# Fixing the order of the tensor engine's instructions in an mLSTM cell followed by a two-layer tanh-shrink block

## Chip, cores and metric

One core of one Trainium2 chip. The metric is the device time of one execution in microseconds (us); times quoted are medians of several executions, and a "span" is the length of the one execution that the profile shows. PE is the tensor engine, PEld its weight loads, DVE, ACT and POOL are the vector, scalar and GpSimd engines.

## The reference

```python
def _attn_ref(q, k, v, i_gate, f_gate, o_gate):          # q, k, v: (4, 8, 768, 40)
    for t in range(S):                                   # ... gates f, i stabilised by a running maximum m
        C = f_stab * C + i_stab * outer(v[t], k[t])      # per batch and head
        n = f_stab * n + i_stab * k[t]
        y[t] = sigmoid(o_gate[t]) * (C @ q[t]) / max(abs(n @ q[t]), 1)

def _moe_ref(x, w_in, w_out):                            # x: (3072, 320), w_in: (320, 2048), w_out: (2048, 320)
    h = x @ w_in
    return (h - np.tanh(h)) @ w_out                      # x is y with heads joined to 320 columns
```

The weights reach the kernel as 64-bit numbers, and it turns them into 32-bit ones itself.

## The kernel before

The cell is done in 24 units of 128 tokens (6 chunks of 128 time steps for each of 4 batches). A unit has, on PE, 8 `scores` calls (tile `ps`), 8 `update` calls of the state (`pc`), 8 `product` pairs (`ph`) and 3 transposes (`px`, which give `xT`). The dense part works on groups of two units: 12 groups of 8 pairs of w_in columns, 6 calls a pair (`ph_up`) and 4 calls of w_out (`po`). The profile has two records a call, except for transposes. `merge` interleaves a quarter of a cell slot with a pair of the dense part by their estimated cost.

```python
V, A, G, T = nc.vector, nc.scalar, nc.gpsimd, nc.tensor
# ...
def weights(dst, src):                    # one piece: 3 pieces a block of w_in, 2 of w_out
    # ... load of 64-bit words, split into lo and hi
    V.tensor_single_scalar(e, hi, 0x7FF00000, op=OP.bitwise_and)
    A.activation(out=e, in_=e, func=AF.Relu, scale=8.0, bias=rebias[0:p])
    V.tensor_single_scalar(m, hi, 12, op=OP.logical_shift_left)
    A.activation(out=mf, in_=m.bitcast(U32), func=AF.Copy, scale=2.0 ** -32, bias=1.0)
    A.activation(out=rf, in_=lo, func=AF.Copy, scale=2.0 ** -52)
    G.tensor_tensor(out=rf, in0=rf, in1=mf, op=OP.add)
    G.tensor_tensor(out=rf, in0=rf, in1=e.bitcast(FP), op=OP.mult)
    V.scalar_tensor_tensor(out=dst.bitcast(I32), in0=hi, scalar=-(1 << 31), in1=r,
                           op0=OP.bitwise_and, op1=OP.bitwise_or)
# ...
xT = [const.tile([128, NK, TG], FP, name=f"xT{i}") for i in range(2)]
# ...
def inter(n):
    def update(h):
        # ...
        T.matmul(t["pc"][:, h, :], t["k"][:, h, :], t["vs"][:, h, :], start=True, stop=True)
    # ...
        steps += [(0.08, lambda h=h: update(h)) for h in range(H)]
# ...
AHEAD = GT + 2
EARLY = 3
for s in range(AHEAD):
    merge(cell_slot(s), convert(s) if s < EARLY else [])
for x in range(len(pairs) + LAG):
    # ... a quarter of a cell slot in `cell`; conversion of block p + EARLY while g == 0
    dense += up(g, p)                     # 6 calls on w_in
    dense += down(*pairs[x - LAG])        # 4 calls on w_out
    merge(dense, cell)
```

The order in the source is not the order that runs: the framework's scheduler reorders each engine's instructions within the dependencies.

Of the kernel before, what the change touches and what calls it, by code (L numbers as in the profile page):

```python
# [34 lines left out]
NO_SYNC = mybir.DependencyInfo(mybir.DependencyClass.NoSync, mybir.DependencyReason.DATA)  # L35
# [14 lines left out]
def kernel(  # L50
# [11 lines left out]
    out: bass.AP,  # L62
):
    nc = tc.nc
    V, A, G, T = nc.vector, nc.scalar, nc.gpsimd, nc.tensor

    B, NT, D, H, _ = qT.shape
    D1 = D + 1
# [91 lines left out]
    for dst, w in ((eS, after), (eT, ones)):  # L160
        p = ps_b.tile([dst.shape[0], NT, BH], FP, name="psum_lf", tag="b")
        T.matmul(p.rearrange("p c n -> p (c n)"), w, lfT.rearrange("p c n -> p (c n)"),
                 start=True, stop=True)
# [158 lines left out]
    def output(n):  # L322


        def accumulate(out, lhsT, rhs, last):
            t = un[n]
            i = T.matmul(out, lhsT, rhs, start=not t["mm"], stop=last, skip_group_check=True)  # L327
            if t["mm"]:
                tc.add_manual_dep(i.ins, t["mm"][-1].ins.name, NO_SYNC, reason="order within a bank")
            t["mm"].append(i)  # L330

        def product(h):
            t = un[n]
            if h == 0:
                t["ph"] = ps_b.tile([L, H, D1], FP, name="ph", tag="b")
                t["mm"] = []
            if t["c"]:
                old = state[t["b"]][t["c"] % 2]
                accumulate(t["ph"][:, h, :], t["qg"][:, h, :], old[:, h, :], False)
            accumulate(t["ph"][:, h, :], t["P"][:, h, :], t["vw"][:, h, :], True)  # L340
            if h == H - 1:
                close()

        def close():
            t = un[n]
            ph, sg = t["ph"], t["o"]
            A.activation(out=sg, in_=sg, func=AF.Sigmoid)

            den = att.tile([L, H], FP, name="den", tag="den")
            V.tensor_scalar(out=den, in0=ph[:, :, D], scalar1=-1.0, scalar2=1.0, op0=OP.mult, op1=OP.max)  # L350
            V.tensor_tensor(out=den, in0=den, in1=ph[:, :, D], op=OP.max)
            V.reciprocal(out=den, in_=den)
            G.tensor_tensor(out=sg, in0=sg, in1=den.unsqueeze(2).to_broadcast([L, H, D]), op=OP.mult)
            y = t["y"] = ys[n % 2]
            V.tensor_tensor(out=y[:, 0:DM].rearrange("p (h d) -> p h d", d=D), in0=ph[:, :, 0:D], in1=sg, op=OP.mult)

        return [(0.44 if n // B else 0.22, lambda h=h: product(h)) for h in range(H)]

    def turn(n):
# [160 lines left out]
```

## Time and profile before

| | before |
|---|---|
| time, median of 4 runs | 745.6 us (744.2 to 745.8) |
| span of the profiled run | 743.2 us |
| PE busy | 674.0 us, 91% |
| last of the 24 w_in pieces converted | 173.2 us |
| PE continuous from | 182.9 us |
| first of the last two output copies starts | 739.3 us, then 3.9 us of tail |

How to read it: before about 183 us PE waits again and again for weights, after it once, for 0.4 us. The prediction below shows the lines. What it and the text below call PE's end (739.3 us) is the start of the first of the last two output copies; by the profile's model PE's last call runs on to 739.8.

### The profile page before, as it was taken

What the parts mean: (1) busy time and instruction counts of PE and PEld (TensorE: products, weight loads), DVE (VectorE), ACT (ScalarE), POOL (GpSimd) and SP (SyncE); (2) the same over time, 40 slices, a digit from 0 to 9 for tenths busy, and PEclk for the clock granted to TensorE, in tenths of its full rate; (3) what the DMA queues carried; (4) which work ended last, traced back from release to release, by engine and by line L of the source; (5) the groups of instructions that cost most, each with busy time, mean ns of one, the idle gap of its engine ahead of it and who ended that gap; (6) DMA issues with size and microseconds to landing.
All of it is one profiled execution on the core that took longest, in us unless ns stands there. A gap on an engine that the chain in (4) does not pass through costs nothing.

```text
span 743.2 us, 9593 instructions
## 1 busy us (share of the span) xinstructions
PE 674.0 (91%) x3418; PEld 531.1 (71%) x3418; DVE 505.5 (68%) x823; ACT 308.7 (42%) x584; POOL 211.5 (28%) x230
## 2 busy tenths in 40 slices
PE   3387756687999999999999999999999999999997
PEld 2375645475787787787787787787787888888885
DVE  8775897488967566666666666666666775656665
ACT  4435644344544334333333333333333444344453
POOL 6467665764011320320320320320320220100000
PEclk8557986679999999999999999999999999999999
DMA  6444544245102121221221111222121000000000
GB/s 187 138 132 136 160 126 129 77 155 158 54 13 79 33 68 54 62 67 53 64 66 54 64 64 54 65 69 76 55 73 37 19 18 27 1 19 1 0 19 18
DMA packets 26487, 50.95 MB, mean 69 GB/s; under 512 B 3304, under 2 KB 15976, under 8 KB 26440
## 3 DMA queue, kind: packets, MB, share of 16 engines
q1 hardware_dynamic: 22568, 46.21, 20.7%
q10 hardware_dynamic: 3872, 4.13, 1.6%
q8 instruction: 27, 0.44, 0.3%
q14 instruction: 20, 0.16, 0.1%
HBM read 46.20 MB, written 4.13 MB: 68 GB/s over the span
## 4 chain that ended last, share of the span: by engine, by line
PE 78%; POOL 9%; DVE 7%; issue 4%; ACT 2%; ACTq 0%; DVEq 0%; POOLq 0%
PE ph_up L401 34%; PE po L430 27%; PE ph L327 9%; PE ps L295 4%; POOL w_r L230 4%; POOL w_r L229 3%; PE pc L309 3%; PE px L367 1%; DVE w_e L223 1%; POOL vw L278 1%; ACT w_m L227 1%; DVE w_in L231 1%; POOL qg L276 1%; DVE w_out L231 1%; ACT w_e L224 1%
## 5 line engine op out<-in xcount | busy, mean ns | idle before, releaser
L401 PE MATMUL ph_up<-xT,w_in 128*128 128x256 f32 x1152 | 325.9, 398 | 17.9 <-DVE w_in L231 15.9
L430 PE MATMUL po<-w_out,gt 128*128 128x320 f32 x768 | 260.6, 454 | 10.7 <-DVE gt L421 8.0
L401 PEld LDWEIGHTS ph_up<-xT,w_in 128*128 128x128 f32 x1152 | 201.6, 194 | 51.4 <-DVE w_in L231 17.0
L413 ACT ACTIVATE z<-ph_up 128x512 f32<-128x512 f32 x96 | 57.3, 597 | 310.4 <-PE ph_up L401 308.6
L430 PEld LDWEIGHTS po<-w_out,gt 128*128 128x128 f32 x768 | 136.2, 194 | 45.3 <-DVE gt L421 8.8
L417 DVE SCALAR_TENSOR_TENSOR w<-ph_up,z 128x512 f32<-128x512 f32 x96 | 65.9, 686 | 118.2 <-ACT t L414 118.2
L295 PEld LDWEIGHTS ps<-qT,kT 128*128 128x128 f32 x384 | 71.9, 223 | 34.8 <-DVE P L297 18.1
L295 PE MATMUL ps<-qT,kT 128*128 128x128 f32 x384 | 74.7, 311 | 24.0 <-DVE P L297 17.3
L308 POOL TENSOR_TENSOR state<-state,eT 40x328 f32<-40x328 f32 x16 | 14.3, 895 | 238.8 <-PE ph L327 232.0
L421 DVE COPY_PREDICATED gt<-big,t 128x512 f32<-128x512 int32 x96 | 74.7, 778 | 7.2
L327 PE MATMUL ph<-vw,P 128*128 128x41 f32 x384 | 77.0, 302 | 0.5 <-ACT xT L369 0.5
L420 DVE SCALAR_TENSOR_TENSOR gt<-q,w 128x512 f32<-128x512 f32 x96 | 72.5, 755 | 5.0 <-DVE den L350 0.4
L327 PEld LDWEIGHTS ph<-state,qg 128*128 128x128 f32 x320 | 61.5, 197 | 15.7 <-POOL w_r L230 1.0
L415 ACT ACTIVATE q<-z,square 128x512 f32<-128x512 f32 x96 | 69.3, 722 | 0.0
L416 ACT ACTIVATE big<-z,border 128x512 f32<-128x512 f32 x96 | 69.0, 719 | 0.0
L419 DVE SCALAR_TENSOR_TENSOR w<-z,w 128x512 f32<-128x512 f32 x96 | 66.9, 697 | 0.0
L418 DVE TENSOR_TENSOR t<-ph_up,t 128x512 f32<-128x512 f32 x96 | 65.3, 680 | 0.0
L278 POOL TENSOR_TENSOR vw<-v,eiT 128x320 f32<-128x320 f32 x24 | 25.4, 1059 | 138.5 <-PE ph L327 92.9
L327 PEld LDWEIGHTS ph<-vw,P 128*128 128x128 f32 x384 | 62.8, 214 | 1.2 <-ACT xT L369 0.9
L414 ACT ACTIVATE t<-ph_up 128x512 f32<-128x512 f32 x96 | 56.8, 592 | 1.6 <-DVE gt L421 1.6
L273 DVE TENSOR_TENSOR_SCAN E<-F,diag 128x1024 f32<-128x1024 f32 x24 | 57.3, 2388 | 0.0
L297 DVE TENSOR_TENSOR P<-ps,E 128x512 f32<-128x512 f32 x48 | 32.5, 682 | 32.7 <-PE ps L295 31.9
(80 smaller groups left out, 528.7 us busy)
## 6 DMA issues: line engine op xcount, KB each, us to landing
F<-f_rows SPq DMA_DIRECT2D x24, 512.0 KB
w<-in_moe_w_out SPq DMA_DIRECT2D x16, 320.0 KB
w<-in_moe_w_in SPq DMA_DIRECT2D x16, 256.0 KB
qT<-in_qT SPq DMA_DIRECT2D x24, 160.0 KB
kT<-in_kT SPq DMA_DIRECT2D x24, 160.0 KB
v<-in_v SPq DMA_DIRECT2D x24, 160.0 KB
k<-in_k SPq DMA_DIRECT2D x24, 160.0 KB
o<-in_o_gate SPq DMA_DIRECT2D x24, 160.0 KB
```

The source lines that it names most:

```text
L273: V.tensor_tensor_scan(out=E.rearrange("p h t -> p (h t)"), data0=t["F"].rearrange("p h t -> p (h t)"), data1=diag.rearrange("p h t -> p ( ...
L295: T.matmul(t["ps"][:, j, :], t["kT"][:, h, :], t["qT"][:, h, :], start=True, stop=True)
L327: i = T.matmul(out, lhsT, rhs, start=not t["mm"], stop=last, skip_group_check=True)
L401: T.matmul(ph[0][:, i, :], w_in[:, j, f * 128:(f + 1) * 128], xT[g % 2][:, j, :], start=(j == 0), stop=(j == NK - 1))
L415: A.activation(out=q, in_=z, func=AF.Square, bias=square)
L416: A.activation(out=big, in_=z, func=AF.Relu, bias=border)
L417: V.scalar_tensor_tensor(out=w, in0=ph, scalar=lead, in1=z, op0=OP.mult, op1=OP.mult)
L418: V.tensor_tensor(out=t, in0=ph, in1=t, op=OP.subtract)
L419: V.scalar_tensor_tensor(out=w, in0=z, scalar=root, in1=w, op0=OP.add, op1=OP.mult)
L420: V.scalar_tensor_tensor(out=gt, in0=q, scalar=rest, in1=w, op0=OP.add, op1=OP.mult)
L421: V.copy_predicated(gt, big.bitcast(I32), t)
L430: T.matmul(po[tt], gT[g, p][:, i, tt * L:(tt + 1) * L], w_out[:, f, :], start=(f == 0), stop=(f == NFF - 1))
```

## The change

The intent is to make PE follow the order of the source: each PE instruction gets a dependency, without a semaphore, on the one issued before it. The scheduler can then no longer move the cell's matmuls against the dense ones, and the first group has to take all its weight columns before the second group starts.

```diff
-    V, A, G, T = nc.vector, nc.scalar, nc.gpsimd, nc.tensor
+    V, A, G = nc.vector, nc.scalar, nc.gpsimd
+
+    class T:
+        last = None
+        @classmethod
+        def keep(cls, i):
+            if cls.last is not None:
+                tc.add_manual_dep(i.ins, cls.last.ins.name, NO_SYNC, reason="order of the tensor engine")
+            cls.last = i
+            return i
+        # matmul and transpose call nc.tensor's and pass the result through keep
@@ accumulate
-            i = T.matmul(out, lhsT, rhs, start=not t["mm"], stop=last, skip_group_check=True)
-            if t["mm"]:
-                tc.add_manual_dep(i.ins, t["mm"][-1].ins.name, NO_SYNC, reason="order within a bank")
-            t["mm"].append(i)
+            T.matmul(out, lhsT, rhs, start=not t["mm"], stop=last, skip_group_check=True)
+            t["mm"] = True
```

More of the change, by code (lines that the diff above doesn't have):

```diff
@@ L64, with matmul, transpose @@
     nc = tc.nc
-    V, A, G, T = nc.vector, nc.scalar, nc.gpsimd, nc.tensor
+    V, A, G = nc.vector, nc.scalar, nc.gpsimd
[7 more added lines that the diff above has]
+            return i
+        @classmethod
+        def matmul(cls, *args, **kwargs):
+            return cls.keep(nc.tensor.matmul(*args, **kwargs))
+        @classmethod
+        def transpose(cls, *args, **kwargs):
+            return cls.keep(nc.tensor.transpose(*args, **kwargs))
     B, NT, D, H, _ = qT.shape
@@ L335, in product @@
                 t["ph"] = ps_b.tile([L, H, D1], FP, name="ph", tag="b")
-                t["mm"] = []
+                t["mm"] = False
             if t["c"]:
```

## The prediction

> **What bounds the kernel now.** I read the busy table first, then the 40 slices, then the stretches, then the tensor engine's timeline. The slices show two regimes:
>
> ```profile
> PE   3387756687999999999999999999999999999997
> ...
> PEclk8557986679999999999999999999999999999999
> ```
>
> A slice is 18.6 us. For ten slices, until about 183 us, TensorE (PE) has gaps and its granted clock wanders between 0.5 and 0.9; after that it is full at full clock to the end. The stretch totals (time; busy us and count of PE, weight load, DVE, ACT, POOL; clock; DMA share; GB/s) say the same:
>
> ```profile
> 20.00:70.00 50.00, 34.71 (x190) 30.23 (x190) 32.38 (x65) 21.96 (x51) 31.61 (x43) 0.59 0.47 145
> 70.00:173.00 103.00, 68.80 (x315) 53.81 (x314) 78.56 (x135) 45.92 (x103) 68.33 (x67) 0.80 0.44 129
> ...
> 183.00:743.00 560.00, 556.32 (x2837) 435.86 (x2837) 369.29 (x576) 225.95 (x406) 95.04 (x88) 1.00 0.15 46
> ```
>
> In the last 560 us PE misses only the tail of 3.9 us: there the end is set by how much PE work is left, and by nothing else. In the first 173 us no engine is full. That stage is the conversion of the 64-bit weights (8 blocks of three w_in and two w_out pieces) passing through DVE, ACT, POOL and DVE in turn, mixed with the cell's own work. The waits (waiter, who it waits for, total us, times, longest) name it:
>
> ```profile
> POOL w_r L229 <- ACT w_m L227: 30.9, 15, 3.9
> ...
> PE ph_up L401 <- DVE w_in L231: 15.9, 7, 6.7
> ```
>
> So the time is: when the last block of w_in is converted, plus the PE work that is still undone then. The tensor timeline around the last block (start, us, what, count of records at two per call, idle before) shows the changeover:
>
> ```profile
> 173.26 3.68 PE L401 MATMUL ph_up<-xT,w_in 128*128 128x256 f32 x8 [3.11 <-DVE w_in L231]
> 176.73 1.82 PE L430 MATMUL po<-w_out,gt 128*128 128x320 f32 x6
> 178.49 0.81 PE L309 MATMUL pc<-vs,k 128*40 128x41 f32 x16
> 179.22 2.05 PE L295 MATMUL ps<-qT,kT 128*128 128x128 f32 x16
> ```
>
> The last piece of w_in lands at 173.2, and from 182.9 PE does not stop.
>
> [...] after the gap at 173 four w_in calls took 176.73 − 173.26 = 3.47 us, 0.87 each, against 0.433 in the steady part. [...] one POOL multiply at 69.62 took 3.06 us, against 0.86 for the same form at 75.42, while DVE ran a scan.
>
> **The change, part by part.** No instruction is added or removed: the dependencies only order PE and need no semaphore. The instruction order of the two builds shows three things.
>
> (1) From the second half of the third group on, the PE order is the same in both, down to the last four cell units, with small shifts only. In the order list the cell matmuls already stand singly between the dense ones there, so "singly between dense ones" is new only in the first two groups. No gain in the steady part.
>
> (2) Until then the scheduler had let PE run ahead: in before, columns of group 1 (the second xT buffer) fill in while group 0 waits for weights, and two more cell units are under way. In the new order group 0 must take all 48 w_in calls, with two cell units between them, before anything of group 1.
>
> (3) POOL's queue up to the last conversion loses 12 cell operations, those of two units (140 lines down to 128).
>
> Cost of (2). I counted calls and took their warm spacing from the steady timeline: w_in call 0.433 us, w_out call 0.539, score 0.22, the pair of output matmuls 0.445, transpose 0.11, state update (pc) 0.396 singly. The last is dear, since pc takes 0.20 itself and makes the following w_in call 0.63 instead of 0.43; bunched, at 178.49, eight took 0.73 us, 0.09 each:
>
> ```profile
> 420.14 0.27 PE L309 MATMUL pc<-vs,k 128*40 128x41 f32 x2
> 420.34 0.70 PE L401 MATMUL ph_up<-xT,w_in 128*128 128x256 f32 x2
> 420.97 0.27 PE L309 MATMUL pc<-vs,k 128*40 128x41 f32 x2
> ```
>
> Check on before: after 182.9 there remain 522 w_in, 356 w_out, 120 scores, 144 pairs, 57 transposes, 104 single pc: 226.0 + 191.9 + 26.4 + 64.1 + 6.3 + 41.2 = 555.9 us. Measured to PE's end (739.26, less a gap of 0.41): 555.9. The count can be trusted.
>
> In the new order, at the end of group 0, there remain 528 w_in, 360 w_out, 144 scores, 152 pairs, 60 transposes, 120 pc: 228.6 + 194.0 + 31.7 + 67.6 + 6.6 + 47.5 = 576.0 us. That is 20.1 us more than before had left at 182.9. So the new kernel ties only if it finishes group 0 by 182.9 − 20.1 = 162.8.
>
> When does it? Group 0's last pair can't finish before the last w_in piece of block 7. After that PE has about 7.0 us of work to the end of the group (4 w_in, 4 w_out, the output pairs), and will be cold after waiting: I add 2 us. So the last w_in must land by about 154, against 173.2 before: the conversion would have to gain 19 us.
>
> What the conversion gains, from (3). The last w_in piece of each block landed in before at 28, 48, 70, 86, 108, 127, 153 and 173. Block 3, with little of the cell in POOL's queue, took 16 us; block 6, with a wait of 4.55 us for PE, vw and vs (1.6), state (1.0) and a qg product of 4.90, took 26. Blocks 0 to 5 keep about the same cell work. Blocks 6 and 7 lose it in the new order, so I give them 17 each instead of 26 and 20: minus 12. Against that, DVE's queue now holds a P product and a shrink (L417) of the current pairs ahead of block 7, which wait for PE, and PE for block 6: I give back 2. Last w_in at 173.2 − 10 = 163, group 0 done at 172, PE at work until 172 + 576 + 0.4 = 748.4, tail 3.9: span 752. Runs show 745.6 for a span of 743.2, so 2.4 more: about 754. I shade to 753[...].
>
> **The rivals.**
> (a) The conversion is much freed: with two fewer units' loads (1.47 MB each by the DMA table) and POOL operations, no run of cold output matmuls ahead of vw (125 to 131 us in before), every block takes 16 us, last w_in at 150. Then the time is about 740. For it: POOL and DVE are no more than 66% and 76% busy in the stretch. Against: the same cells' loads, E scans and P products for units 4 to 6 remain[...].
> (b) A new wait takes the place: PE in strict order waits for a block, the P and shrink behind it hold DVE's queue, DVE holds the next block; so conversion and PE alternate rather than overlap. Four of the remaining blocks at 4 us each would eat the whole gain and more: last w_in at 175, time about 766. [...] Against: in the built DVE queue most of these waits stand 8 to 15 us behind the block that they need.
> (c) The steady part gets better or worse by the order. PE shows no idle time there, and the order is the same, so I expect 0; only if the cells, no longer half a slot ahead, come late could the shrink or xT make PE wait, a few us.
>
> **Range and chances.** The step with all the uncertainty is the landing of the last w_in, 163, give or take 12. That carries over one to one: 741 to 767. Faster by over 2% (below 730.7) needs it at 140, a block rate of 14 us that before never showed: 0.04. Slower by over 2% (above 760.5) needs it at 170 or later, that is nearly no gain from (3): 0.22. Within 2%: 0.74.
>
> **What would show it.** Right: the last w_in conversion between 155 and 170; PE continuous from shortly after, with about 576 us of work from the end of group 0; more idle of PE on w_in than 15.9 us; fewer cell matmuls by then; steady pitch still 27.84 us for a half group with its cell unit. Wrong: last w_in at 153 or earlier (then (a)); POOL and DVE idle more on PE in the first 180 us (then (b)); any idle of PE after 200 us (then (c)).

The sum: 173.2 − 10 = 163 for the last w_in piece, about 172 with 7.0 us of work and 2 of cold cost, + 576 + 0.4 = 748.4, + 3.9 of tail = 752, + 2.4 = about 754, shaded to 753. The 2 us is an estimate from the kernel before: after the gap at 173 four w_in calls took 4 × (0.87 − 0.433) = 1.7 us longer than in the steady part, at a granted clock of 0.51 from 173.3 to 176.7. The output matmuls called cold under (a) ran at 0.50 (125 to 131 us). In a fixed order a matmul waits behind one whose weights aren't converted; the result below shows it, with a wait of 6.32 us.

## The result and the profile after

The changed kernel took 762.3 us (760.5 to 764.1, 4 runs) against 745.6: a ratio of 1.0228, 95% interval 1.0201 to 1.0255, slower by over 2%. A ratio here is the mean time of one kernel's fast runs over that of the other's of the same rounds, so it is not quite the ratio of the medians quoted. The direction and the range held (741 to 767), the forecast of 753 did not: it foresaw 7.4 us of loss, and 16.7 came.

All PE lines of the changed kernel have one line number (L80, transposes L84), as they pass through one helper; the others are shifted by 17 to 19. Its slices and stretch totals, to be laid beside those in the prediction:

```profile
PE   1545883849999999999999999999999999989997
...
PEclk9766886769999999999999999999999999999999
```

```profile
20.00:70.00 50.00, 25.97 (x170) 23.98 (x170) 34.62 (x66) 20.46 (x47) 31.97 (x43) 0.70 0.46 147
70.00:173.00 103.00, 66.77 (x248) 48.52 (x249) 77.83 (x133) 50.86 (x113) 62.19 (x60) 0.72 0.39 124
183.00:743.00 560.00, 557.29 (x2891) 436.16 (x2890) 366.99 (x572) 221.92 (x399) 101.41 (x94) 1.00 0.15 48
```

From 70 to 173 us PE issued 248 records where it had issued 315. That work now lies behind. From 183 us on PE is nearly full in both. PE's wait on w_in grew, as the prediction said. POOL's wait on ACT grew too, from 30.9 to 41.8 us:

```profile
POOL w_r L248 <- ACT w_m L246: 41.8, 16, 4.9
...
PE ph_up L80 <- DVE w_in L250: 25.9, 6, 6.3
```

PE waited 25.9 us on w_in instead of 15.9. Now the last w_in piece, on DVE's timeline (start, us, what, idle before):

```profile
164.07 0.42 DVE L250 SCALAR_TENSOR_TENSOR w_in<-w,w_r 64x256 int32<-64x256 int32 x1 [0.62 <-POOL w_r L249]
```

It lands at 164.5, 8.7 us earlier than before. DVE's timeline bears out the prediction's guess of 17 us each for blocks 6 and 7 (counted from 0): they took 15.2 and 19.4 us (25.5 and 20.4 before), and block 5 landed 2.6 us later. PE's timeline around the last piece, up to the first call of the second group:

```profile
163.50 1.22 PE L80 MATMUL ph_up<-xT,w_in 128*128 128x256 f32 x2 [6.32 <-DVE w_in L250]
164.52 0.49 PE L80 MATMUL ph<-state,qg 128*128 128x41 f32 x2
...
173.48 0.32 PE L80 MATMUL ph<-state,qg 128*128 128x41 f32 x2
...
175.46 0.59 PE L80 MATMUL ph_up<-xT,w_in 128*128 128x256 f32 x2
```

In the first line PE stands idle for 6.32 us behind a w_in call; the cell's `ph` pair behind it has to wait as well, though another pair of its unit had run at 156.34. This is the tie at work. The same call, `ph<-state,qg`, is modelled at 0.49 us until 171.6 and at 0.32 from 173.5. The starts say the same: from it to the next dense call it is 0.72 us at 171.56 and 0.37 at 173.48. PE ran at half clock for 10 us (granted clock 0.50 from 163.5 to 173.5) although it was busy all that time. Group 0 was done at 175.5. Much later, PE's timeline has one wait of this size that the kernel before doesn't have:

```profile
667.06 0.59 PE L80 MATMUL ph_up<-xT,w_in 128*128 128x256 f32 x2
670.37 0.33 PE L84 MATMUL px<-ident,ys 128*128 128x128 f32 x1 [2.71 <-DVE ys L372]
```

The first transpose of the last unit but one stands only one w_out and one w_in call behind the last matmul that its `ys` is made from. There are no scores left to stand between, as there are in earlier slots. The scheduler had set it later.

So PE's end moved from 739.3 to 754.8, by 15.5 us. Counted from the last w_in piece, PE needed 739.3 − 173.2 = 566.1 us before and 754.8 − 164.5 = 590.3 us after, 24.2 more. That is 20.1 of work no longer done ahead (the count of the prediction), 1.3 from a slower finish of the first group (11.0 us from piece to group end, where before had PE continuous 9.7 after the piece), and 2.7 of wait for `ys`: 24.1. The landing gives back 8.7. The medians differ by 1.2 us more than this; the profiled run was the shortest of the four. Its trace lacks something that other traces with this wait have, the slower calls after it (see "The wait at the end").

### The profile page after: what moved, and what is told of

Read it like the earlier page. It is cut to its first block, busy times and chain, and to the rows that moved or that the text cites. A ratio compares the mean times of both kernels' runs of the same rounds, so it can differ in the third digit from the quotient of the medians.

```text
span 758.7 us, 9604 instructions
## 1 busy us (share of the span) xinstructions
PE 675.1 (89%) x3418; PEld 526.4 (69%) x3418; DVE 507.9 (67%) x823; ACT 309.0 (41%) x584; POOL 214.3 (28%) x230
## 3 DMA queue, kind: packets, MB, share of 16 engines
q1 hardware_dynamic: 22568, 46.21, 19.4%
## 4 chain that ended last, share of the span: by engine, by line
PE 79%; DVE 8%; POOL 7%; issue 3%; ACT 2%; DMA 1%; ACTq 0%; SPq 0%; DVEq 0%; POOLq 0%
PE ph_up L80 35%; PE po L80 27%; PE ph L80 8%; PE ps L80 5%; PE pc L80 3%; POOL w_r L248 3%; POOL w_r L249 2%; DVE w_e L242 1%; DVE E L292 1%; PE px L84 1%; DVE w_in L250 1%; ACT w_e L243 1%; ACT w_m L246 1%; POOL vw L297 1%; DVE w_out L250 1%
## 5 line engine op out<-in xcount | busy, mean ns | idle before, releaser
L80 PE MATMUL ph_up<-xT,w_in 128*128 128x256 f32 x1152 | 340.5, 404 | 31.6 <-DVE w_in L250 25.9
L80 PE MATMUL po<-w_out,gt 128*128 128x320 f32 x768 | 265.8, 455 | 3.6 <-DVE gt L438 3.6
L80 PEld LDWEIGHTS ph_up<-xT,w_in 128*128 128x128 f32 x1152 | 199.2, 196 | 60.2 <-DVE w_in L250 21.0
L80 PEld LDWEIGHTS po<-w_out,gt 128*128 128x128 f32 x768 | 133.2, 194 | 32.7 <-DVE gt L438 4.3
L80 PEld LDWEIGHTS ps<-qT,kT 128*128 128x128 f32 x384 | 74.8, 211 | 28.1 <-DVE P L316 14.7
L80 PE MATMUL ps<-qT,kT 128*128 128x128 f32 x384 | 76.6, 297 | 13.7 <-DVE P L316 13.7
L80 PE MATMUL ph<-vw,P 128*128 128x41 f32 x384 | 75.0, 292 | 0.0
L80 PEld LDWEIGHTS ph<-state,qg 128*128 128x128 f32 x320 | 62.2, 194 | 17.2 <-issue 0.8
L80 PEld LDWEIGHTS ph<-vw,P 128*128 128x128 f32 x384 | 61.7, 206 | 1.6 <-issue 0.4
L80 PEld LDWEIGHTS pc<-vs,k 128*40 128x40 f32 x320 | 23.8, 123 | 52.2 <-issue 51.4
```

What stands on the lines that cost most here:

```text
L80: return cls.keep(nc.tensor.matmul(*args, **kwargs))
```

## The experiments

Theory: the loss is made in the start. A cell matmul tied behind a dense one that waits for weights can't fill that wait (6.32 us at 163.5 above), and its work is done later, when PE has no time to spare (557.29 of 560 us busy from 183 on). Rivals: the fixed order costs something by itself in the steady part; it is the ban on columns of the second group; the cell stands too late in the source.

### Order fixed from the third group on

```diff
+            if not cls.on:
+                cls.last = None
+                return i
@@ loop over pairs
+        T.on = x >= 2 * NP
```

While the chain is off, the dependency within a bank of the kernel before is kept; so in all runs that leave something free.

> The order of the tensor engine is fixed only from the third group of columns on (where both kernels have almost the same order anyway); in the first two groups the scheduler is free again, as in the kernel before. Theory (all of the loss is made in the start, plus up to 2.7 us at the very end from one transpose that waits for ys): 743 to 749 us, the last w_in piece at about 173, the tensor engine continuous from about 183. Rival (the fixed order costs by itself, also in the steady part): about 760 us.

Measured: 752.3 us, ratio 1.0076 (1.0048 to 1.0105); last w_in piece at 173.7. Nearer to the theory than to the rival, but 3 us above its range. Its timeline says where that comes from:

```profile
178.96 0.81 PE L84 MATMUL pc<-vs,k 128*40 128x41 f32 x16
183.38 5.38 PE L84 MATMUL ph_up<-xT,w_in 128*128 128x256 f32 x16 [3.60 <-DVE t L441]
...
661.49 0.33 PE L88 MATMUL px<-ident,ys 128*128 128x128 f32 x1 [2.72 <-DVE ys L378]
```

Before, eight scores stood between the `pc` and the `ph_up` here (16 records at 179.22 in the prediction's lines). They now lie past the seam where the chain begins: about 1.8 us of work later (8 × 0.22). PE stood idle for 3.6 us instead of 1.6, and then did the next eight calls in 188.59 − 183.38 = 5.2 us instead of 3.5. With 0.5 for the later piece and 2.7 for the wait at 661 that is 6.7 us, against 6.5 in the medians. In the profiled run, the longest of the four, PE's end came 8.3 us later; the other 1.7 us went by between that wait and PE's end, 86.1 us instead of 84.4 (below). So my range left out the seam; in the steady part the order costs nothing but the one wait and what follows it.

### Order fixed in the first two groups only

The same edit with `T.on = x < 2 * NP`.

> The complement: the order is fixed only in the first two groups of columns and left to the scheduler after that. Theory (start alone): 758 to 761 us, that is the changed kernel less the 2.7 us wait at the end. Rival (the steady part costs): about 747 us.

Measured: 760.5 us (758.3 to 764.1), ratio 1.0191 (1.0142 to 1.0239). As the theory said. No wait for `ys` is left near the end, but in the profiled run the last w_in piece came 2.7 us later than in the changed kernel, so this run alone doesn't show what the wait is worth. The start scatters from run to run: in the two profiles of the changed kernel itself the piece landed at 164.5 and 166.1.

### Only the dense matmuls chained

```diff
@@ up and down, ahead of their T.matmul
+            T.on = True
@@ keep
+            if not cls.on:
+                return i
+            cls.on = False
```

> Only the dense matmuls (w_in and w_out) are chained, so the first group still has to take all of its columns before the second group may start; the cell matmuls may be brought forward by the scheduler. Theory A (of the 20.1 us of work that the kernel before had done ahead, about 15.5 is that of cell units brought forward, and only 4.8 dense): close to before, 744 to 752 us. Theory B (it is the dense columns of the second group that filled the waiting): about 757 to 762 us.

Measured: 752.3 us, ratio 1.0076 (1.0046 to 1.0107), at the edge of theory A's range and well below theory B's. PE's timeline:

```profile
168.25 1.22 PE L84 MATMUL ph_up<-xT,w_in 128*128 128x256 f32 x2 [4.03 <-DVE w_in L254]
173.57 3.78 PE L84 MATMUL ph_up<-xT,w_in 128*128 128x256 f32 x8 [4.10 <-DVE w_in L254]
```

The last piece lands at 173.5 as before, but PE waits 4.0 and 4.1 us for w_in with nothing of the second group to do. Freeing the cell alone takes back 10 of the 16.7 us, 2.7 of them or more at the end, as the wait for `ys` is gone as well. Chaining the dense calls costs the other 6.6. That is more than the ban on the second group's columns: when the second group begins at 180.0, the count has 565.5 us of work left, 9.7 more than before had at 182.9. Of that, 4.8 is dense and 4.9 is cell work (8 scores and 8 updates) that the scheduler didn't bring forward here. The start 2.9 us sooner gives part of it back.

### Only the cell's matmuls chained

The same flag turned round: dense calls outside the chain, cell calls among themselves in the order of the source.

> The complement of the run that chained the dense matmuls alone: here only the cell's matmuls are chained among themselves, and the dense ones are free, so a cell matmul may again pass a dense one that waits for weights. Counted from the order list, the work left after the last call of the first group is 558.5 us, against 555.9 in the kernel before. Theory (what costs is the coupling of cell and dense, not either order): 746 to 752 us, the last w_in piece at 170 to 175. Rival (any fixing costs): about 757 us or more.

Measured: 747.4 us (5 rounds), ratio 1.0019 (0.9999 to 1.0040): as good as before. The rival is out. PE's timeline:

```profile
169.22 1.78 PE L84 MATMUL po<-w_out,gt 128*128 128x320 f32 x6
175.22 3.78 PE L84 MATMUL ph_up<-xT,w_in 128*128 128x256 f32 x8 [4.22 <-DVE w_in L254]
...
180.00 1.00 PE L84 MATMUL pc<-vs,k 128*40 128x41 f32 x16
181.59 2.83 PE L84 MATMUL ph_up<-xT,w_in 128*128 128x256 f32 x12 [0.59 <-DVE t L442]
```

The last piece lands even later, at 175.2, 10.7 us after the changed kernel's. Yet PE ends at 744.6 − 3.9 = 740.7, 565.5 us after it, instead of 590.3. PE also waited only 13.4 us on w_in (25.9 in the changed kernel). At the very start its PE waits 11.9 us for `lf`, as in the changed kernel (1.8 before), so that wait isn't what costs. The order of the cell alone is harmless or nearly so, that of the dense calls alone costs 6.6 us. If these add up, the other 8.4 of the 16.7 us come only when the two are tied together while one of them waits, 2.7 or more of them as the wait at the end.

### Two more cell units ahead, order fixed

```diff
-    xT = [... for i in range(2)]
+    xT = [... for i in range(3)]          # and g % 3 where it is used
-    AHEAD = GT + 2
-    EARLY = 3
+    AHEAD = GT + 4
+    EARLY = 4
```

> The changed kernel, order still fixed, but with the cell started two units earlier against the dense part (lead 6 units instead of 4, four blocks converted during the lead instead of three, a third xT buffer). Theory: the work left at the end of the first group falls by two units, some 17 us, and the conversion loses most of the 8.7 us that it had gained, so 747 to 757 us. Rival (a fixed order can't use the waiting, wherever the cells stand): 760 us or more.

Measured: 759.3 us (754.6 to 759.7), ratio 1.0166 (1.0130 to 1.0202). A miss: I had thought that two units cost the conversion 9 us. DVE's timeline shows what they cost:

```profile
84.49 0.93 DVE L250 SCALAR_TENSOR_TENSOR w_in<-w,w_r 64x256 int32<-64x256 int32 x1 [1.34 <-POOL w_r L249]
...
118.57 0.42 DVE L250 SCALAR_TENSOR_TENSOR w_in<-w,w_r 64x256 int32<-64x256 int32 x1 [0.61 <-POOL w_r L249]
...
179.99 0.42 DVE L250 SCALAR_TENSOR_TENSOR w_in<-w,w_r 64x256 int32<-64x256 int32 x1 [1.03 <-POOL w_r L249]
```

The fifth block takes until 119.0 instead of 105.6 in the changed kernel, and the last piece lands at 180.4, 15.9 us later, for 16.8 us less from there to PE's end. The exchange is nearly one to one, so little is won: 3 us in the medians. (From the transpose after the wait for `ys` to the w_in call behind the next four w_out calls it is 7.44 us in this trace, 628.68 to 636.12, and 4.59 in the changed kernel's, 670.37 to 674.96: about 3 us more.) Part of it is the edit's own: the lead now has two slots without a conversion step in them, where it had one. That a better placed lead would also win nothing is not shown.

### The conversion shortened in both kernels

```diff
@@ weights, after the load
+        V.tensor_single_scalar(dst.bitcast(I32), hi, 0, op=OP.bitwise_or)
+        return
```

Their outputs are wrong, which doesn't matter for the times. First the kernel before, then the changed one:

> The kernel before with the chain of weight conversion cut to one DVE operation a piece (a wrong result on purpose; the loads stay). Alone it says where the time goes to without the conversion: from about 70 us on the tensor engine has some 626 us of work, so 690 to 710 us. To be compared with the next run.

> The changed kernel with the same shortened conversion (wrong on purpose). Theory (the loss is work that PE can't do while it waits for w_in): the difference from the run before this one falls from 16.7 to at most 9 us, of which 2.7 is the wait for ys at the end and up to 5.7 the state updates now standing singly in the first groups. Rival (the order itself costs, whatever the conversion does): the difference stays near 16 us.

Measured: 693.7 us (median of four with one slow run; fast runs 689.8 to 695.6) and 702.3 us (702.1 to 702.8), ratios to the kernel before of 0.9284 and 0.9417. Their difference, 0.0133 of 745.6, is 9.9 us, against 16.7 with the full conversion. The rival's 16 is out, though 9.9 is a little over the 9 that I had allowed, and the first of the two scatters by 6 us. Its profiled run was a slow one, so I don't read its trace against the other. Of the 9.9, the wait for `ys` is in the trace of the changed one:

```profile
610.33 0.33 PE L84 MATMUL px<-ident,ys 128*128 128x128 f32 x1 [2.72 <-DVE ys L374]
```

The calls after it run slow, which costs another 1.7: from this transpose to the w_in call behind the next four w_out calls it is 6.27 us (610.33 to 616.60), against 4.59 in the changed kernel's first profile (670.37 to 674.96; next section). What the other 5.5 us are made of is open; my estimate for the singly standing state updates of the first groups was up to 5.7.

### The wait at the end: the changed kernel again, and without it

The changed kernel ran again as a neighbour, unaltered, and then with one transpose group outside the chain:

> The changed kernel once more, unaltered, so that the next run has a neighbour on the same chip: 760 to 764 us by both theories.

```diff
-            T.transpose(t["px"][:, j, :], ...)
+            (nc.tensor if n == NU - 2 else T).transpose(t["px"][:, j, :], ...)
```

> The changed kernel with one transpose group (three px transposes, those of the last unit but one) left out of the fixed order; the scheduler then sets them some 3 us of matmuls later, every other tensor engine call stands as before. Theory (the 2.71 us wait for ys delays the end one to one): the wait is gone from the trace and the time is 2.7 us below the run before this one, 757 to 761 us. Rival (the dense work behind it then waits for something else, or the start's scatter hides it): within 1 us of the run before this one.

Measured: the changed kernel 762.0 us, ratio 1.0212 (1.0187 to 1.0237); without the wait 758.3 us, ratio 1.0178 (1.0156 to 1.0201). The ratios differ by 0.0034, or 2.5 us, and the medians by 3.7, though the intervals overlap. The trace is plainer. The order differs in these calls alone, and PE runs through:

```profile
667.54 2.75 PE L80 MATMUL ph_up<-xT,w_in 128*128 128x256 f32 x12
670.13 0.70 PE L80 MATMUL po<-w_out,gt 128*128 128x320 f32 x2
670.86 0.44 PE L384 MATMUL px<-ident,ys 128*128 128x128 f32 x2
```

The trace of the changed kernel's second series has the same wait, and shows that it can cost more than itself. After the wait the five w_in calls take 3.27 us, from 671.95 to the next transpose; in the first profile of the same kernel they take 2.16 (670.54 to 672.70):

```profile
671.79 0.33 PE L84 MATMUL px<-ident,ys 128*128 128x128 f32 x1 [2.72 <-DVE ys L372]
671.95 3.47 PE L80 MATMUL ph_up<-xT,w_in 128*128 128x256 f32 x10
675.22 0.42 PE L84 MATMUL px<-ident,ys 128*128 128x128 f32 x1
```

To the w_in call behind the next four w_out calls it is 6.27 us here (671.79 to 678.06) and 4.59 there (670.37 to 674.96). From the transpose to PE's end it is 86.1 us here, in the run ordered from the third group on and in the changed kernel with the shortened conversion, but 84.4 in the first profile, where the clock stays at 1.00: 1.7 us more. So the wait costs 4.4 us in these three traces and 2.7 in the first.

### State updates bunched

The prediction noted that a `pc` standing alone between dense calls takes 0.396 us, and one in a bunch 0.09. Both kernels have over 100 of them alone in the steady part. The edit issues the eight of a unit as one step:

```diff
-            steps += [(0.08, lambda h=h: update(h)) for h in range(H)]
+            steps += [(0.64, lambda: [update(h) for h in range(H)])]
```

First in the changed kernel:

> The changed kernel with the eight state-update matmuls of a unit issued together instead of one at a time between dense calls. From the steady part: singly 0.396 us each, bunched about 0.09. Theory (a single one costs what the spacing says, and the tensor engine sets the end from 175 us on): 120 times 0.3 = 36 us less, so 722 to 730 us. Rival (the spacing is only latency that another engine would set anyway, or bunching makes the dense matmuls wait for the state): 755 us or more.

Measured: 727.2 us, ratio 0.9739 (0.9707 to 0.9771). 35 us less than the changed kernel, where 36 were expected. The eight, on PE's timeline of this run:

```profile
409.62 0.81 PE L80 MATMUL pc<-vs,k 128*40 128x41 f32 x16
410.36 2.43 PE L80 MATMUL ph_up<-xT,w_in 128*128 128x256 f32 x10
```

0.74 us for all eight. Then the same edit in the kernel before:

> The kernel before (order left to the scheduler) with the eight state-update matmuls of a unit as one step. The 104 single ones after 182.9 us cost 41.2 us, bunched some 9.4, so about 31 us less: 712 to 718 us, and below the changed kernel with the same edit (727.2) by about 10 to 14 us. Rival (bunching gained in the changed kernel only because its order was bad): no better than 727.

Measured: 722.8 us, ratio 0.9684 (0.9658 to 0.9710). Better than the last, but 5 us short of my range. The edit had moved the start: the last w_in piece lands at 177.6 instead of 173.2, and PE has a new gap:

```profile
179.50 1.78 PE L430 MATMUL po<-w_out,gt 128*128 128x320 f32 x6
184.03 1.28 PE L309 MATMUL pc<-vs,k 128*40 128x41 f32 x16 [2.75 <-issue]
```

So I kept the order of the start, and bunched only the units after it:

```diff
-            steps += [(0.08, lambda h=h: update(h)) for h in range(H)]
+            if n < 7:
+                steps += [(0.08, lambda h=h: update(h)) for h in range(H)]
+            else:
+                steps += [(0.64, lambda: [update(h) for h in range(H)])]
```

> The kernel before with the state updates bunched only from the eighth unit on, so that its order in the first 180 us is kept (bunching all of them had moved the last w_in piece from 171 to 177). Work left after the start by the count: 529.2 us, against 560.0 in the kernel before. Theory: 30.8 us less than before, 713 to 717 us, and 6 to 9 us less than with all bunched. Rival (the later start with all bunched was scatter): about 722 us.

Measured: 716.4 us (716.2 to 717.7), ratio 0.9608 (0.9594 to 0.9623). As expected, and the best of all (the pieces named as 171 and 177 in the expectation land at 173.2 and 177.6): 29 us below the kernel before, 46 below the changed one. The last w_in piece lands at 173.5. The weight loads of `pc` show what is gone (busy us, mean ns, idle just before them and what ended it), in the kernel before

```profile
L309 PEld LDWEIGHTS pc<-vs,k 128*40 128x40 f32 x320 | 22.3, 125 | 41.9 <-issue 41.2 <-POOL qg L276 0.4
```

and in this one:

```profile
L309 PEld LDWEIGHTS pc<-vs,k 128*40 128x40 f32 x320 | 15.6, 127 | 7.6 <-issue 4.0 <-POOL qg L276 3.0 <-POOL w_r L230 0.3
```

The load path stood idle ahead of the 40-column loads for 41.9 us in sum, 41.2 of it waiting for nothing that the profile shows; now it is 7.6. One such load takes 125 ns in the mean, a 128-column load of w_in calls 194 (kernel before). With 104 of the 160 calls bunched, 0.28 us was gained for each (745.7 − 716.4 = 29.3 us).

## Why the prediction was right or wrong

**Right: the mechanism and the count.** The work left at the end of the first group was put at 576.0 us. From 175.5 to PE's end at 754.8 the trace has 579.3, less the waits of 2.7 and 0.4: 576.2. (With the modelled end of the last call both this and the check on the kernel before are 0.5 us longer; the count is good to that.) That the conversion would gain, but less than what is lost, was right too; of the rivals, neither (a), a much freed conversion (the last piece by 150), nor (b), a conversion held up (175), came; POOL waited for PE 6.5 us in the first 180 us, 10.9 before. The fixed order in the first two groups is the main cause: alone it gives 760.5. Of the signs named, the landing between 155 and 170, more idle on w_in, fewer cell matmuls done and the steady pitch came true (in steady stretches 96 records of `ph_up` every 55.68 us in both kernels, twice 27.84). The sign against it, idle of PE after 200 us, came too, and it pointed at the right rival, (c).

**The step that failed** is the sum under "What the conversion gains": "Last w_in at 173.2 − 10 = 163, group 0 done at 172, PE at work until 172 + 576 + 0.4 = 748.4". Three of its terms were mis-sized, all the same way:

- "PE has about 7.0 us of work to the end of the group ... and will be cold after waiting: I add 2 us". Measured 11.0 instead of 9: 2.0 us. I took the cold cost from before, where the half clock ended 3.4 us after PE took up work (0.51 from 173.3 to 176.7); here it lasted 10 us (0.50 from 163.5 to 173.5).
- Rival (c), "PE shows no idle time there, and the order is the same, so I expect 0". Measured 2.7 us, the wait for `ys`, in the profiled run. The "small shifts" that I had seen in the order list near the end were not harmless. Taking the shift of that one group away took the wait away.
- The conversion's gain, 10 us. Measured 8.7, a landing at 164.5 instead of 163: 1.5 us.

With 0.2 in the count they are the 6.4 us between 748.4 and 754.8. The rest of the miss isn't in the terms of the sum: the shade and rounding downwards took 1.7 us that I had worked out (748.4 + 3.9 + 2.4 = 754.7, recorded as 753), and the median run was 1.8 us longer than the profiled one (the 1.7 us of slower calls after the wait would fit, but no trace of a median run shows it), less 0.6 of the 2.4 allowed between span and run. 6.4 + 1.7 + 1.8 − 0.6 = 9.3, the miss from 753 to 762.3. The shade had the wrong sign.

The range rested on the same mistake: "the step with all the uncertainty is the landing of the last w_in", and over 760.5 was to need it at 170 or later. It came at 164.5, and the time was over 760.5 all the same, by the terms above, which the range left out. One reading of the clock is cut from the prediction: in the kernel before, half clock (0.51 from 173.3 to 176.7) followed a gap of 3.11 us; how long a gap has to be for that is not shown.

**Wrong in emphasis:** the prediction named columns of the second group first among what had filled the waiting. By its own counts the cell units are about 15.5 of the 20.1 us and dense work of the second group 4.8. Freeing only the cell took back 10 us of 16.7; freeing only the dense calls, which frees the cell against them as well, took back all but 1.7. Both sums hold the wait at the end, which neither run has.

**What stays open:** why PE ran at half clock for 10 us while busy (163.5 to 173.5; in the second profile 165.2 to 174.4), where the kernel before had 3.4 us of it; why the calls after the wait for `ys` ran slower in some traces (after 2.72 us of wait in the second profile) and not in the first (after 2.71 us, at a clock of 1.00); and some 5.5 us between the two kernels with the shortened conversion.

## What to carry to other kernels

Where two streams share one engine and one of them waits for something slow, leave their relative order free until the slow thing is over; fixing the order of the cell alone cost nothing clear here and that of the dense calls alone 6.6 us, tying the two together 16.7 us. In the stage where one engine is full, look for calls that cost more than their own time: here a small matmul between large ones took 0.40 us, half of it in the call after it, and 0.09 in a bunch. Bunching eight of them was worth more (29 us) than the whole question of order. When a list of instruction order shows "small shifts", ask for each moved instruction what it waits for and when that is ready.
